# The last group's rows dealt to four column chunks: every fourth row, loaded by sixteen turns, stored and read back in 3328-byte pieces

## The chip, the cores and the metric

The kernel runs on one core of a Trainium2 chip. The metric is the time of one execution on the device in microseconds (us), the median of several runs. Beside these runs there is one execution taken with the hardware profiler; "the span" is the time from its first to its last instruction.

## The reference

A cross network (DCN) with six layers over 16384 rows of 416 bf16 features:

```python
B, F, D, L = 16384, 26, 16, 6          # Din = F * D = 416
def reference(x0, ws, bs):
    x = x0
    for l in range(L):
        proj = jnp.einsum('bd,de->be', x, ws[l]) + bs[l]
        x = x0 * proj + x
    return x
```

The inputs are `x0` of 16384 x 416, `ws` of 6 x 416 x 416 and `bs` of 6 x 416; the output has the shape of `x0`.

## The kernel before

The rows are cut into eight groups of 2048 (GC), each group into four chunks of 512 columns (NJ = 4, CH = 512). Inside the core a group stands transposed: features on the partitions, rows along the free dimension. The 416 features are three tiles of 128 (NT = 3) and a tail of 32. The tails of the four chunks share one tile of 128 partitions, one quadrant of 32 partitions to a chunk.

**Loading.** `load_group(g)` transposes a group while it loads it, by DMA transposes from the SP queue, here called turns. Each turn takes 2048 rows of 128 features: one for each feature tile (L408), and one of the last 128 features into a buffer `Tb`, which shares its memory with the output buffer `ost` (L413). Four small DMAs (L420) then copy the tails from `Tb` to their quadrants, and for some groups two more DMAs (L445, L446) write a rotated copy of the tails. The input buffers are five slots used in turn; group 7, the last, uses slot 2. Its load is queued when group 2 has been done with.

**Computing.** Jobs are pairs of group and layer. Matmuls for most of the run are issued in an order written out by hand (`ORDER`, replayed by `replay` and `stream`). A chunk's result is moved from PSUM by ScalarE with the bias added (L551), multiplied with x0 by VectorE (L563) and added to x (L568). The buffers of x are a pool of six (`xs`), those of the tails a pool of ten; a buffer that a finished group gives back is taken by a later job. The small rotations of tails (L445, L446) between layers also go through SP.

**Output of groups 0 to 4.** `output(g)` turns the finished features back to rows by four DMA transposes within SBUF (`turn`, L892, and `turn_rest`, L899), GpSimd spreads the tails (L922), and `store` writes the 2048 rows (L929). A row is 832 bytes. For group 0, whose rows were dealt to partitions four at a time when it was loaded, a partition writes 3328 bytes in one piece; for the other groups a piece is one row.

**The last layer of group 7.** It is computed the other way round, with rows on the partitions, so that no turn is needed after it. The group is handled in row blocks `kk` = 0 to 3, each with four PSUM banks j = 0 to 3: ScalarE copies a bank to `on` (L1189), VectorE multiplies with x0 in row-major form, `x0n7` (L1195), and adds x in row-major form, `x5n` (L1201), and `nat_store` writes the rows (L1208). Blocks 0 to 2 are one store each, block 3 is a store of half a block and two of a quarter. Group 6's last half is stored (L929) between them.

**Row-major x0.** `load_last()` reads group 7's x0 a second time, as rows (L870, four DMAs of 0.416 MB), into slot 3, and the last layer's bias (L874, four small DMAs). It is called when group 3 has been done with, right behind that group's turns and store in SP's queue. `on` uses slot 4, `x5n` slot 0.

A column of chunk j stands for a row of the group: with c the column's number in the chunk, before it is row 512 j + c.

The wait counts, and which engine waits for what, are worked out by `Program` from the names of tiles that each operation reads and writes; every engine's queue keeps the order in which operations were added.

Of the kernel before, what the change touches and what calls it, by code (L numbers as in the profile page):

```python
# [3 lines left out]
P = 128  # L4
CH = 512
# [16 lines left out]
class Program:  # L22
# [12 lines left out]
    def add(self, eng, fn, reads=(), writes=(), lane=None, batch=None, hold=False, release=False, row=None):  # L35
        op = Op(eng, fn, lane, batch, row)
        deps = {}
        if eng == "pool":
            writes = list(writes) + ["pool"]
        for t in reads:  # L40
            w = self.writer.get(t)
            if w is not None:
                deps[id(w)] = (w, True)
        for t in writes:
            w = self.writer.get(t)
            if w is not None:
                deps[id(w)] = (w, True)
            for r in self.readers.get(t, ()):
                if id(r) not in deps:
                    deps[id(r)] = (r, False)  # L50
        for d, raw in deps.values():
            if d.lane is None and d.eng == eng and lane is None and (eng == "pe" or not raw):
                if row is None or d.row is None or row == d.row:
                    continue
            op.deps.append(d)
        for t in reads:
            self.readers.setdefault(t, []).append(op)
        for t in writes:
            self.writer[t] = op
            self.readers[t] = []  # L60
        if eng == "dve":
            if hold:
                self.flush()
                self.held = op
            else:
                self.queue[eng].append(op)
                if release:
                    self.flush()
        else:
            self.queue[eng].append(op)  # L70
        if lane is not None:
            batches = self.lanes.setdefault(lane, [])
            if not batches or batches[-1][0] != batch:
                batches.append((batch, []))
            batches[-1][1].append(op)
        return op
# [230 lines left out]
def bass_standalone__cross_network_dcn__recsys_kernel(  # L307
# [6 lines left out]
    B, D = x0.shape  # L314
    L = ws.shape[0]
    NT = 3
    NJ = 4
    GC = NJ * CH
    NG = B // GC
    KK = CH // P  # L320
    assert D == NT * P + T32 and B == NG * GC and NG == 8 and L == 6
    LAST = NG - 1
# [10 lines left out]
    n = 0  # L333
# [6 lines left out]
    XW = NT * GC  # L340
# [7 lines left out]
    x0s = [nc.alloc_sbuf_tensor(f"x0_{s}", [P, XW + 2 * CH], BF16) for s in range(NX0)]  # L348
# [4 lines left out]
    ost = nc.alloc_sbuf_tensor("ost", [P, GC // P, D], BF16)  # L353
    Tb = ost[:, :, :].rearrange("p a f -> p (a f)")[:, 0:GC]
# [4 lines left out]
    add = pr.add  # L359
# [4 lines left out]
    def x0_tok(s, t, j):  # L364
        return ("x0", s, t, j)

    def x0_all(s):
        return [x0_tok(s, t, j) for t in range(NT) for j in range(NJ)] + [("x03r", s), ("x03r", s, "b")]
# [4 lines left out]
    def slot(g):  # L373
        return g % NX0
# [29 lines left out]
    def load_group(g):  # L404
        s = slot(g)
        rows = slice(g * GC, (g + 1) * GC)
        def turn(t):
            add("sp", lambda h: h.dma_start_transpose(  # L408
                x0s[s][:, t * GC:(t + 1) * GC], x0[rows, t * P:(t + 1) * P]),
                writes=[x0_tok(s, t, j) for j in range(NJ)], lane=f"x0_{s}_{t}", batch=g)  # L410

        turn(0)
        add("sp", lambda h: h.dma_start_transpose(Tb, x0[rows, D - P:D]),  # L413
            writes=[("ost", t, j) for t in range(NT + 1) for j in range(NJ)], lane="Tb", batch=g)
        turn(1)
        turn(2)
        if g > 1:
            for j in range(NJ):
                q = slice(j * T32, (j + 1) * T32)
                add("sp", lambda h, q=q, j=j: h.dma_start(  # L420
                    x0s[s][q, XW:XW + CH], Tb[P - T32:P, j * CH:(j + 1) * CH]),
                    reads=[("ost", 0, 0)], writes=[("x03q", s, j)], lane=f"x03_{s}", batch=g)
            rotate_x03(g)

    def rotate_x03(g):
        s = slot(g)
        if turn_of(g, 1):
            rotate(x0s[s][:, XW:XW + CH], x0s[s][:, XW + CH:XW + 2 * CH], turn_of(g, 1),
                   x03_toks(s), ("x03r", s), f"x03r_{s}", g)

    def x03_toks(s):
        return [("x03q", s, j) for j in range(NJ)]
# [23 lines left out]
    def x_src(g, l):  # L456

        if l == 0:
            s = slot(g)
            return lambda t, a, b: x0s[s][:, t * GC + a * CH:t * GC + b * CH], lambda t, j: x0_tok(s, t, j)  # L460
        s = xset[(g, l)]
        return lambda t, a, b: xs[s][:, t * GC + a * CH:t * GC + b * CH], lambda t, j: ("x", s, t, j)
# [8 lines left out]
    def done_with(g, l):  # L471
        users[(g, l)] = users.get((g, l), 0) + 1
        if users[(g, l)] < 2:
            return
        if l > 0:
            free_x.append(xset[(g, l)])
            free_3.append(xtail[(g, l)])
        if (g, l + 1) not in filled:
            prefill(g, l + 1)
        if l == L - 1:  # L480
            output(g)
            if g == 3:
                load_last()
            if 4 < g + NX0 <= LAST:
                later.append(g + NX0)
# [133 lines left out]
    def prefill(g, l):  # L619

        if 0 < l < L and turn_of(g, 1) and (g, l) != (LAST, L - 1):
            so = free_3.pop(0)
            xtail[(g, l + 1)] = so
            n = (turn_of(g, l + 1) - turn_of(g, l)) % NJ
            rotate(x3s[xtail[(g, l)]], x3s[so], n, [("x3", xtail[(g, l)])], ("x3", so), f"rot{so}", (g, l))
# [46 lines left out]
    def tails(batch, corners_last=False, banks=None):  # L672
# [42 lines left out]
        for g, l in batch:  # L715
            done_with(g, l)
        while later:
            load_group(later.pop(0))
# [6 lines left out]
        out=ident[:, :], in_=ident[:, :], compare_op=ALU.not_equal, fill=1.0, base=0,  # L725
# [8 lines left out]
    def load_nat(j, k0, k1):  # L734
# [6 lines left out]
        reads=["warm"], writes=["warm"])  # L741
# [6 lines left out]
    load_w3(0, "sp")  # L748
    load_wm(0, "sp", W0, D)
    load_group(1)  # L750

    def second_tails():
# [108 lines left out]

    view = "p (j k f) -> p j k f"
    sn, so, s5 = slot(3), slot(4), slot(5)
    x0n7, x5n, on = (x0s[s][:, 0:XW + CH].rearrange(view, j=NJ, k=KK) for s in (sn, s5, so))
    rows7 = x0[LAST * GC:B, :]

    def load_last():

        for j in range(NJ):
            add("sp", lambda h, j=j: h.dma_start(  # L870
                x0n7[:, j, :, :], rows7[j * CH:(j + 1) * CH, :].rearrange("(k p) f -> p k f", k=KK)),
                writes=(x0_all(sn) + x03_toks(sn) if j == 0 else []) + [("n7", j)], lane="n7", batch=0)
        for j in range(NJ):
            add("sp", lambda h, j=j: h.dma_start(brow[j * T32:j * T32 + 1, :], bs[L - 1:L, :]),  # L874
                reads=["brow"], writes=[("brow", j)], lane="brow", batch=0)

    def output(g):

        s, s3 = xset[(g, L)], xtail[(g, L)]
        if g < LAST - 2:  # L880
            turn(g, 0)
            turn_rest(g)
            spread("pool")
            turn(g, 1)
            turn(g, 2)
            store(g, 0, NJ)
        free_x.append(s)
        free_3.append(s3)
# [72 lines left out]
    k = 0  # L961
# [17 lines left out]
    def start_job(g, l, ahead=True):  # L979
        started.add((g, l))  # L980
        if ahead:
            xset[(g, l + 1)] = free_x.pop(0)
        if (g, l) in W_LOAD:
            load_wm(W_LOAD[(g, l)], "sp")
            load_w3(W_LOAD[(g, l)], "sp")
        if (g, l) in G_LOAD:
            load_group(G_LOAD[(g, l)])
# [141 lines left out]
    g, l = LAST, L - 1  # L1129
    src, stok = x_src(g, l)  # L1130
# [61 lines left out]
    def nat_mul(kk, j, n=2):  # L1192
        o, x0v = on[:, j:j + n, kk, :], x0n7[:, j:j + n, kk, :]
        toks = [("on", a, kk) for a in range(j, j + n)]
        add("dve", lambda h: h.tensor_tensor(o, o, x0v, ALU.mult),  # L1195
            reads=toks + [("n7", a) for a in range(j, j + n)], writes=toks)

    def nat_add(kk, j, n=2):
        o, x5v = on[:, j:j + n, kk, :], x5n[:, j:j + n, kk, :]
# [4 lines left out]
    stores = [0]  # L1204

    def nat_store(kk, j0, j1, eng="sp"):
        dst = out[LAST * GC:B, :].rearrange("(j k p) f -> p j k f", j=NJ, k=KK)[:, j0:j1, kk, :]
        add(eng, lambda h: h.dma_start(dst, on[:, j0:j1, kk, :]),  # L1208
            reads=[("on", j, kk) for j in range(j0, j1)],
            writes=[("out7", kk, j0)], lane=f"out7_{stores[0]}", batch=0)  # L1210
        stores[0] += 1
# [18 lines left out]
    for j in (0, 2):  # L1230
        nat_mul(0, j)
    for j in (0, 2):
        nat_add(0, j)
    nat_store(0, 0, NJ)
    store(LAST - 1, 2, NJ)
    for kk in range(1, KK):
# [48 lines left out]
```

## Time and profile before

| what | us |
|---|---|
| median of 3 runs | 466.94 |
| lowest and highest | 466.86, 467.11 |
| the profiled execution | 467.6 |
| its span | 465.8 |
| busy: TensorE, VectorE, ScalarE, GpSimd | 459.0, 402.9, 382.3, 6.9 |
| first and last start of L408 turns | 7.4, 285.3 |
| from issue to landing: L408, L413, L899 (median) | 5.2, 6.0, 2.6 |
| from issue to landing: stores L929, L1208 (median) | 7.1, 4.3 |

TensorE's granted clock was 0.998 over the span. The DMA engines moved 53.78 MB, a mean of 115 GB/s; of 139152 packets 112826 are under 512 bytes, most of them the turns' 256. In views of the trace, "SPq" and "ACTq" are the DMA issues of SP and ScalarE; the time beside such a line is how long the issue held the queue, not how long the data took. "DMA share" is the mean busy share of the 16 DMA engines in a stretch; it can stand a little above 1, since packets overlap.

### The profile page before, as it was taken

The page shows a single profiled execution, that of the slowest core. Times are in us where ns is not written, and L with a number is a line of the kernel's source. Part 1 is how long each engine was busy: PE and PEld are TensorE (multiplying, and loading weights), DVE is VectorE, ACT ScalarE, POOL GpSimd, SP SyncE. Part 2 cuts the span into 40 slices and gives each one's busy share as a digit, 9 for nine tenths or more (in the row PEclk, how much of TensorE's full clock was granted, in tenths as well). Part 3 has the DMA queues.
Part 4 walks back from the last instruction along what each step waited for, and adds up shares of the span by engine and source line. Part 5 has one row for each costly group of instructions (what it writes and reads, how often), then busy time and mean ns, then how long its engine had stood idle before and what let it go on. Part 6 is the DMA issues. An engine that isn't in the chain of part 4 may idle for free.

```text
span 465.8 us, 17814 instructions
## 1 busy us (share of the span) xinstructions
PE 459.0 (99%) x8001; PEld 265.9 (57%) x8001; DVE 402.9 (87%) x696; ACT 382.3 (82%) x609; POOL 6.9 (1%) x15
## 2 busy tenths in 40 slices
PE   9999999999999999999999999999999999999994
PEld 5344656575655556555665556565556665556552
DVE  1887898988889898898988979898988988989996
ACT  4686889887988888897888889888888897989794
POOL 1000000000000000000000000000000000000000
PEclk9999999999999999999999999999999999999999
DMA  8985859000002859095568619983000084182999
GB/s 229 185 177 120 176 118 193 10 23 12 16 4 37 152 172 189 13 143 167 110 120 126 183 36 177 132 239 115 25 2 4 25 148 149 37 137 82 184 177 275
DMA packets 139152, 53.78 MB, mean 115 GB/s; under 512 B 112826, under 2 KB 138564, under 8 KB 139076
## 3 DMA queue, kind: packets, MB, share of 16 engines
q1 hardware_dynamic: 138920, 52.54, 52.8%
q8 instruction: 62, 1.02, 0.9%
q10 hardware_dynamic: 156, 0.11, 0.1%
q14 instruction: 14, 0.11, 0.1%
HBM read 5.97 MB, written 13.63 MB: 42 GB/s over the span
## 4 chain that ended last, share of the span: by engine, by line
PE 96%; DVE 2%; ACT 1%; issue 0%; DVEq 0%
PE ps L1075 73%; PE ps L692 7%; PE ps L1079 6%; PE ps L645 5%; PE ps L639 1%; PE ps L680 1%; DVE x L1201 1%; DVE x L1195 1%; PE ps L772 1%; PE ps L790 1%; ACT tw L551 1%; PE ps L666 1%; DVE tw L563 0%; DVE x L568 0%; DVE x L1163 0%
## 5 line engine op out<-in xcount | busy, mean ns | idle before, releaser
L1075 PE MATMUL ps<-x,wm 32*128 32x512 bf16 x6288 | 372.9, 374 | 0.0
L551 ACT ACTIVATE tw<-ps,bias 128x512 bf16<-128x512 f32 x524 | 327.3, 688 | 48.6 <-PE ps L1075 35.9
L1075 PEld LDWEIGHTS ps<-x,wm 32*128 32x128 bf16 x6288 | 221.6, 92 | 136.0 <-ACT tw L551 6.5
L563 DVE TENSOR_TENSOR tw<-tw,x 128x1024 bf16<-128x1024 bf16 x262 | 176.6, 687 | 41.5 <-ACT tw L551 40.0
L568 DVE TENSOR_TENSOR x<-tw,x 128x1024 bf16<-128x1024 bf16 x262 | 171.0, 688 | 0.3
L1079 PE MATMUL ps<-x,w 32*128 32x512 bf16 x524 | 159.3, 374 | 0.0
L1079 PEld LDWEIGHTS ps<-x,w 32*128 32x128 bf16 x524 | 44.6, 92 | 6.1
L692 PE MATMUL ps<-x,wm 128*32 128x512 bf16 x564 | 33.6, 380 | 0.0
L612 ACT ACTIVATE ts<-ps,bias 128x512 bf16<-128x512 f32 x32 | 20.4, 686 | 13.1 <-PE ps L680 13.1
L515 ACT ACTIVATE tw<-ps,bias 128x1024 bf16<-128x1024 f32 (+1 forms) x24 | 20.7, 938 | 8.1 <-PE ps L666 7.0
L692 PEld LDWEIGHTS ps<-x,wm 128*32 128x32 bf16 x564 | 13.5, 96 | 18.2 <-ACT tw L551 3.7
L645 PE MATMUL ps<-x,wm 128*128 128x512 bf16 x92 | 21.6, 384 | 0.0
L616 DVE TENSOR_TENSOR x<-ts,x 128x512 bf16<-128x512 bf16 x47 | 18.4, 418 | 0.3
L645 PEld LDWEIGHTS ps<-x,wm 128*128 128x128 bf16 x92 | 8.4, 98 | 11.7 <-issue 2.3
L524 DVE TENSOR_TENSOR tw<-tw,x 128x1024 bf16<-128x1024 bf16 (+1 forms) x21 | 13.0, 636 | 2.2 <-ACT tw L515 2.1
L608 DVE SCALAR_TENSOR_TENSOR ts<-ps,bias,x 128x512 bf16<-128x512 f32 x15 | 11.2, 747 | 3.1 <-PE ps L680 3.1
L529 DVE TENSOR_TENSOR x<-tw,x 128x1024 bf16<-128x1024 bf16 (+1 forms) x21 | 12.6, 633 | 0.0
L614 DVE TENSOR_TENSOR ts<-ts,x 128x512 bf16<-128x512 bf16 x32 | 12.4, 417 | 0.0
L922 POOL COPY ost<-ot 128x512 bf16<-128x512 bf16 x6 | 5.5, 912 | 390.8 <-DMA ot<-x 390.8
L800 DVE COPY x<-ps 128x512 bf16<-128x512 bf16 x5 | 2.0, 423 | 8.6 <-PE ps L790 8.6
L1140 PE MATMUL ps<-wm,x 128*128 128x416 bf16 x48 | 9.3, 340 | 0.0
L1189 ACT ACTIVATE x<-ps 128x416 bf16<-128x416 f32 x16 | 7.7, 528 | 1.5 <-PE ps L1140 1.5
(51 smaller groups left out, 72.7 us busy)
## 6 DMA issues: line engine op xcount, KB each, us to landing
out_dram<-ost SPq DMA_DIRECT2D x6, 1664.0 KB, 7.8
x<-x SPq DMA_DIRECT2D x24, 96.0 KB, 2.2
x<-in_x_dram SPq DMA_DIRECT2D x8, 208.0 KB, 4.5
x<-in_x_dram SPq DMA_DIRECT2D x4, 416.0 KB, 8.3
out_dram<-ost SPq DMA_DIRECT2D x2, 832.0 KB, 4.2
wm<-in_ws_dram SPq DMA_DIRECT2D x5, 312.0 KB, 3.4
x<-x SPq DMA_DIRECT2D x22, 64.0 KB, 2.2
out_dram<-x SPq DMA_DIRECT2D x3, 416.0 KB, 4.9
```

The source lines that it names most:

```text
L515: add("act", lambda h, a=a, w=w, b0=b0: h.activation(tw[r][:, a * CH:(a + w) * CH], psum[:, b0 * CH:(b0 + w) * CH], ACT_F.Identity, bias=b ...
L524: add("dve", lambda h, a=a, e=e: h.tensor_tensor(tw[r][:, a * CH:e * CH], tw[r][:, a * CH:e * CH], x0s[s0][:, i * GC + a * CH:i * GC + e * ...
L529: add("dve", lambda h, a=a, e=e: h.tensor_tensor(xs[so][:, i * GC + a * CH:i * GC + e * CH], tw[r][:, a * CH:e * CH], src(i, a, e), ALU.ad ...
L551: add("act", lambda h: h.activation(tw[r][:, j * CH:(j + 1) * CH], bank(b), ACT_F.Identity, bias=bias[:, i, l:l + 1], scale=1.0), reads=[( ...
L563: add("dve", lambda h: h.tensor_tensor(tw[r][:, o], tw[r][:, o], x0s[s0][:, c], ALU.mult), reads=[("tw", r, k) for k in both] + [x0_tok(s0 ...
L568: add("dve", lambda h: h.tensor_tensor(xs[so][:, c], tw[r][:, o], src(i, a, a + 2), ALU.add), reads=[("tw", r, k) for k in both] + [stok(i ...
L612: add("act", lambda h: h.activation(ts[r][:, :], bank(b), ACT_F.Identity, bias=bias[:, 3, l:l + 1], scale=1.0), reads=[("ps", b), "bias"], ...
L616: add("dve", lambda h: h.tensor_tensor(x3s[so][:, :], ts[r][:, :], res, ALU.add), reads=[("ts", r)] + rtok, writes=[("x3", so), ("x3", so, ...
L645: add("pe", lambda h, t=t, j=j: h.matmul(bank(banks[j]), wm[l][:, t, ecols], src(t, j, j + 1), start=(first and t == 0), stop=(not first a ...
L692: add("pe", lambda h, t=t, j=j, src=src, l=l, b=b, ro=ro, qo=qo: h.matmul(psum[qo, b * CH:(b + 1) * CH], wm[l][:, t, NT * P:D], src(t, j, ...
L1075: add("pe", lambda h, l=l, t=t, j=j, b=b, q=q, ecols=ecols, src=src, kw=kw: h.matmul(bank(b), wm[l][q, t, ecols], src(t, j, j + 1)[q, :], ...
L1079: add("pe", lambda h, l=l, b=b, q=q, ecols=ecols, s3=s3, kw=kw: h.matmul(bank(b), w3[l][q, ecols], s3[q, :], **kw), reads=tok3 + [("w3", l ...
```

## The change

Group 7's rows are dealt out anew: column c of chunk j is now row 4 c + j of the group. So a partition of a row block holds four neighbouring rows in its four banks.

For this the group's load takes every fourth row: each of its four turns becomes four, of 512 rows each, one to a chunk, with a stride of four rows in DRAM (16 turns in all). `x0n7` and `on` change their layout in SBUF, so that the four rows of a partition stand side by side, 3328 bytes; `x5n` keeps its own. `load_last` now makes one DMA for each row block, with 128 pieces of 3328 bytes, and is called when group 4 has been done with, not group 3. `nat_store` writes a partition's rows in one piece: 3328 bytes for row blocks 0 to 2, 1664 for the first half of block 3, 832 as before for its last two quarters. VectorE's multiply at L1195 names all four of the row-major loads as read.

```diff
     def load_group(g):
...
+        by4 = x0[rows, :].rearrange("(q j) f -> j q f", j=NJ)
+
         def turn(t):
-            add("sp", lambda h: h.dma_start_transpose(
-                x0s[s][:, t * GC:(t + 1) * GC], x0[rows, t * P:(t + 1) * P]),
-                writes=[x0_tok(s, t, j) for j in range(NJ)], lane=f"x0_{s}_{t}", batch=g)
+            if g < LAST:
+                add("sp", lambda h: h.dma_start_transpose(
+                    x0s[s][:, t * GC:(t + 1) * GC], x0[rows, t * P:(t + 1) * P]),
+                    writes=[x0_tok(s, t, j) for j in range(NJ)], lane=f"x0_{s}_{t}", batch=g)
+                return
+            for j in range(NJ):
+                add("sp", lambda h, j=j: h.dma_start_transpose(
+                    x0s[s][:, t * GC + j * CH:t * GC + (j + 1) * CH], by4[j, :, t * P:(t + 1) * P]),
+                    writes=[x0_tok(s, t, j)], lane=f"x0_{s}_{t}", batch=g)
+
+        def turn_b(j0, j1, src):
+            add("sp", lambda h: h.dma_start_transpose(Tb[:, j0 * CH:j1 * CH], src),
+                writes=[("Tb", j) for j in range(j0, j1)] + (
+                    [("ost", t, j) for t in range(NT + 1) for j in range(NJ)] if j0 == 0 else []), lane="Tb", batch=g)
 
         turn(0)
-        add("sp", lambda h: h.dma_start_transpose(Tb, x0[rows, D - P:D]),
-            writes=[("ost", t, j) for t in range(NT + 1) for j in range(NJ)], lane="Tb", batch=g)
+        if g < LAST:
+            turn_b(0, NJ, x0[rows, D - P:D])
+        else:
+            for j in range(NJ):
+                turn_b(j, j + 1, by4[j, :, D - P:D])
         turn(1)
         turn(2)
...
             output(g)
-            if g == 3:
+            if g == 4:
                 load_last()
...
-    x0n7, x5n, on = (x0s[s][:, 0:XW + CH].rearrange(view, j=NJ, k=KK) for s in (sn, s5, so))
+    x5n = x0s[s5][:, 0:XW + CH].rearrange(view, j=NJ, k=KK)
+    x0n7, on = (x0s[s][:, 0:XW + CH].rearrange("p (k j f) -> p j k f", j=NJ, k=KK) for s in (sn, so))
...
-        for j in range(NJ):
-            add("sp", lambda h, j=j: h.dma_start(
-                x0n7[:, j, :, :], rows7[j * CH:(j + 1) * CH, :].rearrange("(k p) f -> p k f", k=KK)),
-                writes=(x0_all(sn) + x03_toks(sn) if j == 0 else []) + [("n7", j)], lane="n7", batch=0)
+        for k in range(KK):
+            add("sp", lambda h, k=k: h.dma_start(
+                x0n7[:, :, k, :], rows7[k * CH:(k + 1) * CH, :].rearrange("(p j) f -> p j f", j=NJ)),
+                writes=(x0_all(sn) + x03_toks(sn) if k == 0 else []) + [("n7", k)], lane="n7", batch=0)
...
     def nat_store(kk, j0, j1, eng="sp"):
-        dst = out[LAST * GC:B, :].rearrange("(j k p) f -> p j k f", j=NJ, k=KK)[:, j0:j1, kk, :]
+        dst = out[LAST * GC:B, :].rearrange("(k p j) f -> p j k f", j=NJ, k=KK)[:, j0:j1, kk, :]
```

More of the change, by code (lines that the diff above doesn't have):

```diff
@@ L421, in load_group @@
                     x0s[s][q, XW:XW + CH], Tb[P - T32:P, j * CH:(j + 1) * CH]),
-                    reads=[("ost", 0, 0)], writes=[("x03q", s, j)], lane=f"x03_{s}", batch=g)
+                    reads=[("ost", 0, 0), ("Tb", j)], writes=[("x03q", s, j)], lane=f"x03_{s}", batch=g)
             rotate_x03(g)
@@ L1195, in nat_mul @@
         add("dve", lambda h: h.tensor_tensor(o, o, x0v, ALU.mult),
-            reads=toks + [("n7", a) for a in range(j, j + n)], writes=toks)
+            reads=toks + [("n7", k) for k in range(KK)], writes=toks)
     def nat_add(kk, j, n=2):
```

## The prediction

> **What bounds the kernel now.** I read the page first, for who carries the span.
>
> ```profile
> PE 459.0 (99%) x8001; PEld 265.9 (57%) x8001; DVE 402.9 (87%) x696; ACT 382.3 (82%) x609; POOL 6.9 (1%) x15
> ...
> PE 96%; DVE 2%; ACT 1%; issue 0%; DVEq 0%
> ```
>
> TensorE is busy 99% of the span and makes up 96% of the chain that ended last. The program's TensorE, VectorE, ScalarE and GpSimd queues hold the same operations in the same order after the change, so nothing up to about 446 us moves unless a transfer comes late. That leaves two places: the end, where no matmul runs any more, and SP's queue, where the transfers are issued. For the end I read the windows.
>
> ```profile
> core 0: us, PE busy (x) PEld busy (x) DVE busy (x) ACT busy (x) POOL busy (x), PEclk, DMA share, GB/s
> 163.00:166.00 3.00, 3.00 (x68) 1.28 (x59) 2.75 (x5) 1.95 (x4) 0.00 (x0) 1.00 1.01 399
> 307.00:310.00 3.00, 3.00 (x61) 1.97 (x56) 2.76 (x6) 2.65 (x6) 0.00 (x0) 1.00 1.05 347
> 459.00:464.00 5.00, 0.75 (x5) 0.20 (x2) 2.39 (x8) 1.28 (x3) 0.00 (x0) 1.00 1.07 343
> ```
>
> The last two columns matter. From 459 to 464 the 16 DMA engines are full (share 1.07) at 343 GB/s. What they move are stores in 832-byte pieces: the second half of group 6 (L929, issued at 457.37) and the row-major stores of the last group (L1208). The row at 307 is another 832-byte store, of group 3, at 347 GB/s. The row at 163 is group 0's store, the only one in 3328-byte pieces: 399 GB/s. The last arithmetic is VectorE's at 461.4, the last data packet ends at 464.6, the span ends at 465.8. So it is the drain of the stores that sets the last four microseconds.
>
> For the queue I read SP's timeline around the group 7 load.
>
> ```profile
> 277.32 2.13 SPq L408 DMA_TRANSPOSE x<-in_x_dram  x1
> 279.50 2.43 SPq L413 DMA_TRANSPOSE ost<-in_x_dram  x1
> 281.98 5.91 SPq L408 DMA_TRANSPOSE x<-in_x_dram  x2
> 287.93 3.34 SPq L420 DMA_DIRECT2D x<-ost  x4
> ...
> 293.74 2.82 SPq L892 DMA_TRANSPOSE ost<-x  x1
> 296.60 1.27 SPq L899 DMA_TRANSPOSE ot<-x  x1
> 297.91 5.05 SPq L892 DMA_TRANSPOSE ost<-x  x2
> 305.83 0.39 SPq L929 DMA_DIRECT2D out_dram<-ost  x1
> 306.27 5.56 SPq L870 DMA_DIRECT2D x<-in_x_dram  x4
> ```
>
> The load's four turns hold SP for 10.6 us, and group 3's output turns (L892, L899) follow with no pause: whatever the load gains in length, they inherit.
>
> **The stores.** Six stores of L1208 change. The first (row block 0) is issued at 454.53, ahead of the half-group L929 store, whose packets start only at 458.3 because it is issued at 457.37; a faster first store leaves a longer gap there and moves nothing. From 458.3 the drain is unbroken. Row blocks 1 and 2 are 0.426 MB each: 1.242 us at 343 GB/s, 1.068 us at 399, so 0.17 us saved on each. The first half of row block 3 goes from 832 to 1664-byte pieces: 0.213 MB, 0.62 us now; no store in the trace has that size, so its gain lies between 0 and 0.09 us (the 3328-byte rate), and I take 0.07, since it is nearer the long piece in what it saves of piece count (a half against three quarters). The last two stores hold one row of 832 bytes per partition as before: nothing. Sum 0.42 us, if the drain stays unbroken: the last store is issued by ScalarE at 461.46, and L929 shows 0.9 us from issue to first packet, so it is ready at 462.4, before its turn comes at about 463.5. It is still the drain that ends last. VectorE's multiplies and adds over 832 elements (L1195, L1201, 0.59 us) read one run instead of two; they were at the pace of the 1024-element L563 already (0.69 us), so I give them nothing.
>
> The Trainium skill ("DMA: Bandwidth & Descriptors", section "Where 436 GB/s comes from") speaks against most of this: it holds that transfers between HBM and SBUF are bound near 358 GB/s per core. By that, the 1.065 MB above would go from 3.11 to 2.97 us, an estimate of 0.13 us saved. The 399 GB/s row of this trace disagrees with it, and I go by the row.
>
> **The sixteen turns.** Four turns of 2048 rows become sixteen of 512. No row shows a 512-row turn from DRAM. The nearest is L899, a turn of 128x512 within SBUF: 1.19 us least, 1.27 median, 2.14 most, the last behind a full queue. The bounds: a 512-row turn as a quarter of the shortest whole L408 (1.67/4 = 0.42 us), or as costly as a whole one here (2.6). I take the median, since the packets of a quarter turn need only about a quarter of 2.6 = 0.65 us of the DMA engines, so the queue behind it shouldn't fill. With the 0.04 us between issues: 16 x 1.31 = 21.0, so SP is 10.4 us later at L420 and after. Ends: earlier by 3.2, at 0.46 each, if the engines' 0.65 does not hold it back to about no change; later by 31 at 2.6.
>
> Who notices 10.4 us? Matching the trace's records to the queues in order:
> Group 7's inputs are first read by TensorE at 315.4. The last turn would be issued by 298.3 and landed by 301 to 304 (2.6 us as L899, 6.1 as now). Covered.
> Group 3's output turns land at 298.6, 304.2 and 305.8. VectorE overwrites what they read in the L568 operations that start at 314.43, 317.84 and 320.27. At 10.4 us later 5.4, 3.3 and 4.1 us are left. Covered; the tightest cover ends at 13.7 us.
> The rotation of group 7's tails (L445, L446 at 292.56) is wanted by VectorE at about 329. Covered. GpSimd's copy (L922) waits for the L899 turn and goes with it, and has nothing behind it until 377. Group 3's store (305.83) goes to 316.2; the output buffer is wanted at 372.
>
> **The residual load.** L870 and L874 (4 + 4 DMAs, 7.5 us of SP) move from behind group 3's store to behind group 4's, past the two pairs of rotations at 313.83 to 316.40, the pairs at 330, 331, 363 and 365, and group 4's turns and store (372.28 to 384.0). The rotations at 313.83 would be issued at 316.7 instead (10.4 later, 7.5 earlier) and wait behind 5 us of group 3's store; they land near 324 and are first wanted at 329.9. At the new place the eight DMAs run from 384.0 to at most 391.6; SP's next operation waits for VectorE until 395.57. Their data follow group 4's store, which lands at 392.0, and need 4.3 us at 399 GB/s; the first reader is L1195 at 452.4. Nothing moves there. The rotations at 395.57 may land a microsecond later; they are wanted from 420.
>
> **Sum.** The profiled execution took 467.6 us with a span of 465.8, 0.7 above the median of the runs. 467.6 - 0.42 = 467.2; on the median, 466.94 - 0.42 = 466.5 us.
>
> **Rivals.** *The drain is no faster.* 399 GB/s was seen with nothing behind it in the queue; at the end small stores and two issuing engines mix. Then the time is 466.9. For it: 832-byte stores too differ by their moment, 347 GB/s at 307 and 308 GB/s between 385.5 and 390. Against: 399 holds for three steady microseconds. 0.15. The Trainium skill's bound (same page and section) would make it 466.8, an estimate.
>
> *A quarter turn is dear* (the other side). One mechanism: SP's delay makes group 3's output turns land after VectorE wants their buffer; VectorE stands at L568 at 317.84 with the L563 multiplies queued behind it; ScalarE's L551 finds its result buffer unread (it reuses them from 7.2 us after); then no PSUM bank comes free and TensorE stands. VectorE waits from a mean of 1.52 us per turn (16 m - 10.6 > 13.7), TensorE from about 1.97 (7.2 more). At 2.18, the dearest L899 row plus its gap, the loss is 16 x 2.18 - 10.6 - 13.7 - 7.2 = 3.4 us: 469.9 us. At 2.6 it is 10: 477. For it: that one row, and that L892 took up to 4.3 us when turns were queued. Against: six of the seven L899 rows are at most 1.71. 0.12, with 0.03 more for a loss in another place that I do not see. It ends slower than before by 0.2% only from a mean of about 2.05 us.
>
> *More than the drain.* If the shorter end also let the half-group store start earlier, which I see no way for, or the freed DMA engines at 307 to 318 helped: over 0.93 us faster, 0.05.
>
> *The change doesn't do what it says*: if a store in the new layout were still cut in 832-byte pieces the result is the first rival's; the built program names 128x1664 for it, so I fold it in there.
>
> **How the numbers follow.** Forecast 0.65, drain no faster 0.15, dear turns 0.12 and elsewhere 0.03, much faster 0.05. 0.2% is 0.93 us, about what a measurement of this kernel can tell from no change; the forecast and the first rival both lie within it: same 0.80, slower 0.15, faster 0.05. The range: below, twice the saving, 466.1; above, no gain and half a microsecond of a stall begun, 467.5. It holds the forecast and the first rival.
>
> **What would show it.** In the profile after: SP's timeline with sixteen turns at about 1.3 us and L892 of group 3 near 304; VectorE's L568 at 314 to 320 with no wait on a DMA; the windows from 459 on near 370 GB/s with the share still full; the last data near 464.2. A TensorE gap near 318 or a VectorE wait there would make the second rival right; a drain at 343 GB/s the first.

## The result and the profile after

The changed kernel takes 466.35 us (median of 17 runs, 465.94 to 466.98) where the kernel before took 467.14 on the same chip (17 runs, 466.86 to 467.47): ratio 0.9983, 95% interval 0.9976 to 0.9991, so 0.4 to 1.1 us faster. The profiled execution took 466.98 us with a span of 465.2, 0.6 us less than before. Line numbers after L404 are higher in the changed kernel, by 8 at first (L408 is L416, L413 is L421), then by 16 (L420 is L436, L568 is L584, L608 is L624) and by 17 (L892 is L909, L929 is L946, L1208 is L1225).

From the page of the changed kernel, the engines' busy time (first line of part 1):

```profile
PE 458.9 (99%) x8001; PEld 267.2 (57%) x8001; DVE 403.3 (87%) x696; ACT 381.9 (82%) x609; POOL 7.2 (2%) x15
```

Nothing in the computation has moved. The windows of the changed kernel, with the DMA share and GB/s in the last two columns:

```profile
core 0: us, PE busy (x) PEld busy (x) DVE busy (x) ACT busy (x) POOL busy (x), PEclk, DMA share, GB/s
307.00:310.00 3.00, 3.00 (x64) 1.93 (x61) 2.76 (x5) 2.64 (x6) 0.00 (x0) 1.00 0.96 184
459.00:464.00 5.00, 0.70 (x4) 0.20 (x2) 2.34 (x7) 1.23 (x3) 0.00 (x0) 0.99 1.05 376
```

The row at 459 is the one that the change was about: the engines are about as full as before (1.05 and 1.07) and carry 376 GB/s instead of 343. At 307 the store of group 3 is gone, it now comes at 317.8, and turns run in its place. SP's timeline of the changed kernel shows why:

```profile
277.43 5.19 SPq L416 DMA_TRANSPOSE x<-in_x_dram  x4
282.66 5.71 SPq L421 DMA_TRANSPOSE ost<-in_x_dram  x4
288.41 11.90 SPq L416 DMA_TRANSPOSE x<-in_x_dram  x8
300.36 3.28 SPq L436 DMA_DIRECT2D x<-ost  x4
...
306.12 2.06 SPq L909 DMA_TRANSPOSE ost<-x  x1
308.22 1.71 SPq L916 DMA_TRANSPOSE ot<-x  x1
309.97 4.50 SPq L909 DMA_TRANSPOSE ost<-x  x2
317.83 0.40 SPq L946 DMA_DIRECT2D out_dram<-ost  x1
```

Sixteen turns hold SP from 277.43 to 300.36, 1.43 us each; the copies behind them come 12.4 us later than before, group 3's store 12.0. VectorE's timeline of the same stretch has no wait on a DMA at the three L584 operations:

```profile
314.73 1.28 DVE L584 TENSOR_TENSOR x<-tw,x 128x1024 bf16<-128x1024 bf16 x2
...
317.94 1.29 DVE L584 TENSOR_TENSOR x<-tw,x 128x1024 bf16<-128x1024 bf16 x2
...
320.34 1.29 DVE L584 TENSOR_TENSOR x<-tw,x 128x1024 bf16<-128x1024 bf16 x2
```

It is close, though: the third of group 3's output turns lands at 317.81, and VectorE starts at 317.94.

### The profile page after: what moved, and what is told of

It is laid out like the page before. It is cut to its first block, busy times and chain, and to the rows that moved or that the text cites. A ratio compares the mean times of both kernels' runs of the same rounds, so it can differ in the third digit from the quotient of the medians.

```text
span 465.2 us, 17826 instructions
## 1 busy us (share of the span) xinstructions
PE 458.9 (99%) x8001; PEld 267.2 (57%) x8001; DVE 403.3 (87%) x696; ACT 381.9 (82%) x609; POOL 7.2 (2%) x15
## 4 chain that ended last, share of the span: by engine, by line
PE 94%; DVE 2%; DMA 1%; ACT 1%; SPq 1%; issue 0%; DVEq 0%
PE ps L1092 73%; PE ps L708 7%; PE ps L1096 6%; PE ps L661 4%; PE ps L655 1%; PE ps L696 1%; DMA x<-in_x_dram 1%; DVE x L1218 1%; DVE x L1212 1%; ACT tw L567 1%; PE ps L682 1%; SPq L751 0%; DVE tw L579 0%; DVE x L584 0%; PE ps L806 0%
## 5 line engine op out<-in xcount | busy, mean ns | idle before, releaser
L584 DVE TENSOR_TENSOR x<-tw,x 128x1024 bf16<-128x1024 bf16 x262 | 171.2, 689 | 0.3
L661 PEld LDWEIGHTS ps<-x,wm 128*128 128x128 bf16 x92 | 8.5, 98 | 11.5 <-issue 2.3
L624 DVE SCALAR_TENSOR_TENSOR ts<-ps,bias,x 128x512 bf16<-128x512 f32 x15 | 11.2, 747 | 3.1 <-PE ps L696 3.1
L630 DVE TENSOR_TENSOR ts<-ts,x 128x512 bf16<-128x512 bf16 x32 | 12.4, 418 | 0.0
```

Of the source, the lines that this page charges most:

```text
L584: add("dve", lambda h: h.tensor_tensor(xs[so][:, c], tw[r][:, o], src(i, a, a + 2), ALU.add), reads=[("tw", r, k) for k in both] + [stok(i ...
L661: add("pe", lambda h, t=t, j=j: h.matmul(bank(banks[j]), wm[l][:, t, ecols], src(t, j, j + 1), start=(first and t == 0), stop=(not first a ...
```

## Experiments

The theory: the whole gain is the drain of the stores at the end, through the size of their pieces; the turns and the moved residual load cost and bring nothing, because they are covered. The rivals: the gain comes from the moved residual load, or the turns cost something that hides a larger gain. A second group of kernels asks how much cover there is. Ratios are to the kernel before on the same chip, with 95% intervals. In the first group that kernel took 467.26 us, in the second 467.10, in the third 467.40.

### Which part gains

**The changed kernel again** (`again`).

> The changed kernel once more, on the same chip as the three beside it. Theory (the drain): only the stores after 458.3 us gain; the trace after shows 0.5 us there, so 0.4 to 0.6 us faster than before, ratio about 0.9989. Rival (something besides the drain gains, for example the residual load that no longer runs beside group 3's store): 0.8 us or more, ratio 0.9983 or less, as the first 17 runs gave.

466.55 us, 0.9985 (0.9977 to 0.9994), span 465.2. The difference of the medians, 0.7 us, lies between the two expectations.

**Short pieces** (`short`): the changed kernel, `on` as it was.

```diff
-    x5n = x0s[s5][:, 0:XW + CH].rearrange(view, j=NJ, k=KK)
-    x0n7, on = (x0s[s][:, 0:XW + CH].rearrange("p (k j f) -> p j k f", j=NJ, k=KK) for s in (sn, so))
+    x5n, on = (x0s[s][:, 0:XW + CH].rearrange(view, j=NJ, k=KK) for s in (s5, so))
+    x0n7 = x0s[sn][:, 0:XW + CH].rearrange("p (k j f) -> p j k f", j=NJ, k=KK)
```

> The changed kernel with `on` laid out as before, so that every store of the last group goes in 832-byte pieces again; the dealt rows, the sixteen turns, the moved residual load and its 3328-byte pieces stay. Theory (the drain): the gain goes, ratio to before 0.9995 to 1.0005, and the windows from 459 to 464 are back at 343 GB/s. Rival (the gain comes from the moved load or from the turns): it keeps most of its gain, ratio 0.9985 or less with a drain at 343 GB/s.

467.21 us, 0.9997 (0.9989 to 1.0006). The gain is gone; its interval and that of `again` still overlap a little, so the drain has to bear it out. In this profile the drain began at 457.3, 0.9 us earlier than in that of the kernel before, so the window is shifted:

```profile
458.00:463.00 5.00, 1.21 (x7) 0.48 (x5) 2.85 (x8) 1.73 (x4) 0.00 (x0) 0.89 1.07 343
```

343 GB/s again, as the theory had it. VectorE's multiplies and adds of the last layer take a median of 0.58 to 0.59 us in the kernel before, in the changed one and in `short`, so the layout gains nothing there. Dealt rows, sixteen turns and the moved load are all in this kernel and bring nothing that can be seen.

**The residual load back behind group 3** (`early`).

```diff
-            if g == 4:
+            if g == 3:
                 load_last()
```

> The changed kernel with the residual load back behind group 3's store. Theory (the drain): nobody waits for those transfers in either place, so the time is that of the changed kernel within 0.1 us; SP's rotations of 318 us go to about 324 and land near 331, where VectorE wants the first at 329.8, so a wait of VectorE of about a microsecond may show, without a cost at the end. Rival (the move of the load is what gains): the time of before, or up to 1 us over it.

466.52 us, 0.9987 (0.9978 to 0.9995): the time of the changed kernel. Its drain:

```profile
458.60:463.60 5.00, 0.61 (x4) 0.12 (x2) 2.25 (x7) 1.14 (x3) 0.00 (x0) 0.90 1.04 375
```

and VectorE's waits between 322 and 336, in the order engine, line, what it waited for, us, times, longest:

```profile
DVE tw L579 <- ACT tw L567: 1.0, 3, 0.5
DVE x L632 <- DMA x<-x: 0.9, 1, 0.9
```

The second line is the wait of a microsecond for the late rotation. It costs nothing at the end. Where the load stands is not what gains.

**The turns alone** (`turns`): the kernel before, with group 7's four turns cut in four, neighbouring rows.

```diff
...
+            for j in range(NJ):
+                add("sp", lambda h, j=j: h.dma_start_transpose(
+                    x0s[s][:, t * GC + j * CH:t * GC + (j + 1) * CH], part(j)[:, t * P:(t + 1) * P]),
+                    writes=[x0_tok(s, t, j)], lane=f"x0_{s}_{t}", batch=g)
...
```

> The kernel before with one part of the change alone: group 7 is loaded by sixteen turns of 512 rows, but neighbouring rows, so the dealing, the layouts, the stores and the residual load are as before. Theory: the sixteen turns are covered; SP reaches L420's copies about 12 us later as in the changed kernel (a mean of 1.43 us a turn, whatever the stride of the rows), the time is that of before within 0.1 us, although the rotations behind the residual load now come some 12 us later too (near 326, wanted at 329.8). Rival (the turns cost something that the changed kernel's stores hide): 0.2 to 0.5 us slower than before.

467.39 us, 1.0009 (0.9998 to 1.0020): a cost between nothing and 0.9 us, which this interval does not settle. Sixteen turns of neighbouring rows took 22.9 us of SP (277.17 to 300.02), those of every fourth row in the changed kernel 22.9 as well: the stride cost nothing here.

The trace's packets give the drain to the hundredth in all of these kernels. From the first packet of group 6's second half to the end of the last: 6.42 us in the kernel before, 6.42 in `short`, 6.43 in `turns`; 5.87 in the changed kernel, in `again` and in `early`. From the last packet's end to the end of the span: 1.10, 1.11 and 1.10 against 0.97, 0.90 and 0.97. So 0.55 us are the drain, and 0.13 to 0.2 more come behind it.

### How much cover there is

Three kernels make the delay of SP longer by more turns in group 7's load, into a free part of the output buffer; their results are not used, but the tail copies wait for them. They stand ahead of the last eight of the load's sixteen turns, so half of group 7's inputs come later too.

```diff
                 turn_b(j, j + 1, by4[j, :, D - P:D])
+            spare = ost[:, :, :].rearrange("p a f -> p (a f)")
+            for n in range(3):
+                add("sp", lambda h, n=n: h.dma_start_transpose(
+                    spare[:, GC + n * 512:GC + (n + 1) * 512], by4[n % NJ, 0:512, D - P:D]),
+                    writes=[("spare", n)], lane="spare", batch=g)
...
```

**Three more** (`dose3`).

> The changed kernel with three more turns of 512 rows in group 7's load, into a part of the output buffer that is free then. SP comes 4.3 us later still: 12.4 + 4.3 = 16.7 us. The prediction's covers: VectorE waits from 13.7 us on, so here some 2 to 3 us in all at the L568 operations of 314 to 320; TensorE only from 20.9: the time stays that of the changed kernel within 0.2 us. Rival (the covers are worth nothing more once VectorE waits): 2 to 3 us slower.

**Eight more** (`dose8`).

> The same with eight more turns: SP 12.4 + 11.5 = 23.9 us later. By the prediction's sum VectorE waits about 10 us and TensorE stands for 23.9 - 20.9 = 3 us: 3 us slower than the changed kernel, 469 to 470. Rival (VectorE's lost time is made up by its idle share, and the first reader among TensorE's matmuls is 13 us and more behind): under 1 us slower. Rival on the other side (every later microsecond counts from 13.7): 10 us slower.

**Sixteen more, of 256 rows** (`dose16`).

> The same with sixteen more turns, of 256 rows each. If such a turn holds SP as long as one of 512 rows (1.3 us, a fixed cost), SP is 12.4 + 21 = 33 us later: by the prediction's sum 12 to 13 us slower than the changed kernel, near 479, and TensorE's first read of group 7 at 315.4 still only just covered. If the time goes with the rows (0.7 us), 12.4 + 11 = 23.5 us later and the time is that of the kernel with eight more turns.

| kernel | group 3's store issued, later than before by | time, us | over the changed kernel (466.55) |
|---|---|---|---|
| `again` | 14.2 | 466.55 | |
| `dose3` | 17.5 | 471.49 | 4.9 |
| `dose8` | 22.4 | 478.04 | 11.5 |
| `dose16` | 33.9 | 489.16 | 22.6 |

The medians are of 4, 4 and 2 runs. The expectations drawn from the prediction (no change, 3, 12 to 13) were all wrong, and the rival of `dose3` (2 to 3 us) was too low as well; that of `dose8` (10 us) came nearest. From `dose3` to `dose16` 16.4 us of delay cost 17.7 us, though not by one path, as shown below. `dose3`, whose profile is of its slowest run (472.55 us), is decided by these waits between 316 and 334:

```profile
DVE x L589 <- DMA ost<-x: 6.4, 2, 4.1
...
PEld ps L1097 <- DVE ts L629: 4.3, 1, 4.3
PE ps L1097 <- DVE ts L629: 3.8, 1, 3.8
```

VectorE waits for the output turns as the rival said, but TensorE does not come to stand through ScalarE. It waits for VectorE itself: L629 (L608 before) reads a tail's PSUM bank with VectorE. VectorE's timeline of `dose3`:

```profile
316.81 1.29 DVE L589 TENSOR_TENSOR x<-tw,x 128x1024 bf16<-128x1024 bf16 x2 [2.32 <-DMA ost<-x]
...
323.44 1.29 DVE L589 TENSOR_TENSOR x<-tw,x 128x1024 bf16<-128x1024 bf16 x2 [4.13 <-DMA ost<-x]
...
331.27 0.74 DVE L629 SCALAR_TENSOR_TENSOR ts<-ps,bias,x 128x512 bf16<-128x512 f32 x1
```

and in the kernel before:

```profile
327.13 0.74 DVE L608 SCALAR_TENSOR_TENSOR ts<-ps,bias,x 128x512 bf16<-128x512 f32 x1
```

The operation that ended at 327.87 now ends at 332.01. TensorE's next matmul into that bank stood at 328.10 before, 0.2 us behind, and stands at 332.07 here.

TensorE's stand of 3.8 us is not the whole loss: the span is 5.5 us over that of the changed kernel (470.7 against 465.2). The windows of `dose3` show the rest:

```profile
330.00:340.00 10.00, 7.93 (x116) 4.05 (x119) 8.01 (x16) 5.07 (x9) 0.00 (x0) 0.83 0.13 36
340.00:350.00 10.00, 10.00 (x191) 5.76 (x188) 9.42 (x16) 8.69 (x15) 0.00 (x0) 1.00 0.01 3
```

The third number from the end is the granted clock. Its mean falls to 0.83 behind the stand; in the trace it is 0.5 from 333.03 to 336.44, and 3.4 us at half the clock lose the missing 1.7.

`dose8` and `dose16` hold other paths besides. Waits in `dose8` between 310 and 345:

```profile
PE ps L1097 <- DVE ts L629: 5.8, 1, 5.8
ACT tw L572 <- DVE x L589: 4.7, 2, 3.8
PEld ps L1097 <- ACT tw L572: 3.4, 2, 3.3
```

and in `dose16` between 310 and 350:

```profile
PE ps L1097 <- DMA x<-in_x_dram: 9.5, 2, 5.4
PEld ps L1097 <- DVE ts L629: 6.3, 1, 6.3
```

In `dose8` TensorE also stood 2.8 us through ScalarE, whose L572 waited for VectorE's L589: the prediction's path, here beside the other. In `dose16` 9.5 us of its stands are waits for group 7's own inputs, which the expectation had as just covered. So these two kernels tell what a long delay costs, not that the one bank costs it.

**That one tail on ScalarE** (`tail_act`): `dose3` with the tail bank of job (4,4) emptied by ScalarE.

```diff
-                evacuate_tail(*batch[k], bs_[k], vector=k == 1)
+                evacuate_tail(*batch[k], bs_[k], vector=k == 1 and batch[k] != (4, 4))
```

> The kernel with three more turns (471.5 us, 0.9 to 1.0% over before), with one thing changed: the tail bank of job (4,4), which VectorE empties itself, L608 in the kernel before, 327.1 to 327.9, and TensorE wants 0.2 us later, is emptied by ScalarE here, as its two neighbours are. Theory (VectorE's wait reaches TensorE through this one bank): TensorE's gap of 3.8 us at 332 goes or shrinks below 1 us, VectorE's waits on the output turns stay at about 6 us, and the time falls to 467.5 or less. Rival (it reaches TensorE through ScalarE's result buffers or the input of the next job, as the prediction's sum had it): it stays near 471.

467.04 us, 0.9995 (0.9982 to 1.0008), where `dose3` had 1.0091 (1.0070 to 1.0111). Its waits between 316 and 334:

```profile
DVE x L589 <- DMA ost<-x: 4.1, 1, 4.1
ACT tw L572 <- DVE x L589: 0.9, 1, 0.9
PEld ps L1097 <- ACT ts L633: 0.7, 1, 0.7
```

VectorE still waits 4.1 us here and 0.5 just before 316 (4.6 in all, where about 6 was expected), and TensorE's stand of 3.8 has shrunk to a gap of 0.4, with its clock at 1.00 throughout. In this profile the third output turn landed 1.6 us earlier than in that of `dose3`; that alone would have left a stand of some 2.2 us (an estimate, 3.8 - 1.6). So the path of `dose3` is shown: one bank, emptied by the engine that was made to wait. What is left over the changed kernel, 0.5 us, lies within the intervals.

The same path is at work, small, in the changed kernel itself. Its second profile (`again`), waits between 313 and 331:

```profile
DVE x L584 <- DMA ost<-x: 2.1, 1, 2.1
...
PEld ps L1092 <- DVE ts L624: 0.8, 1, 0.8
```

There the third output turn landed at 320.05, not 317.81, and VectorE waited 2.1 us; its idle time before L624 took up most of that, and TensorE lost 0.3.

### Can the end be shorter still

The DMA engines have nothing to do between 457.9 and 458.3, because group 6's second half waits for its last turn, while row block 1 has been ready since 456.7. `swap` issues row block 1 first; `bswap` does the same to the kernel before; `half` stores row block 1 in two halves as well.

```diff
     nat_store(0, 0, NJ)
-    store(LAST - 1, 2, NJ)
...
         if kk < last:
             nat_store(kk, 0, NJ)
+        if kk == 1:
+            store(LAST - 1, 2, NJ)
```

and for `half`, besides:

```diff
                 nat_add(kk, j - 1)
+                if kk == 1:
+                    nat_store(kk, j - 1, j + 1)
...
-        if kk < last:
+        if 1 < kk < last:
             nat_store(kk, 0, NJ)
```

> The changed kernel with one order changed on SP: the store of row block 1 is issued before the store of group 6's second half, not after it. Theory (the drain sets the end from 456 us on, and the gap of some 0.4 us in the DMA engines at 457.9 to 458.3 is only there because the half-group store waits for its last turn): row block 1 is ready at 456.7, its packets fill the gap, and the end comes 0.4 to 0.7 us sooner than in the changed kernel, ratio to before about 0.997 to 0.998. Rival (the end hangs on the last store's own way from its issue at 461.4, not on the queue of data): no gain over the changed kernel.

> The kernel with the store of row block 1 ahead of group 6's second half once more, beside two of its relatives. First it gave 0.9981 where the changed kernel gave 0.9985 on the same chip, with intervals that overlap. Theory (the idle stretch of the DMA engines before 458.3 is the end's): 0.3 to 0.5 us under the changed kernel's 466.5, ratio 0.9972 to 0.9980. Rival (no gain): 0.9985.

> The kernel before with that swap of two stores alone, 832-byte pieces, nothing dealt anew. Theory: the swap and the long pieces are separate gains of the same queue of data, so here some 0.3 to 0.5 us faster than before, ratio 0.9990 to 0.9994. Rival (only with long pieces is there an idle stretch worth filling): no change, 0.9997 to 1.0003.

> The swap, and row block 1 stored in two halves of 1664-byte pieces, the first as soon as its two banks are done (a microsecond earlier). Theory: the DMA engines' idle half microsecond at 457 goes too, 0.2 to 0.3 us under the swap alone. Rival: the shorter pieces (69 ns against half of 135) and one more issue on SP, 0.6 to 1.2 us each, take it back: the swap's time or 0.2 us over it.

| kernel | time, us | ratio to before | 95% interval |
|---|---|---|---|
| `swap` | 466.14 | 0.9981 | 0.9972 to 0.9990 |
| `swap_again` | 466.50 | 0.9983 | 0.9974 to 0.9992 |
| `bswap` | 467.08 | 0.9999 | 0.9990 to 1.0007 |
| `half` | 466.23 | 0.9980 | 0.9971 to 0.9989 |

Each of the intervals overlaps that of the changed kernel, 0.9977 to 0.9994. In the profiles the idle stretch is shorter (`swap`, 0.24 us) or gone (`swap_again`, `bswap`, `half`), the spans of `swap`, `swap_again` and `half` are 464.6, 464.0 and 464.4 against 465.2, and the engines carry more between 455 and 458. The changed kernel:

```profile
455.00:458.00 3.00, 3.00 (x24) 1.38 (x23) 2.93 (x6) 2.07 (x4) 0.00 (x0) 1.00 0.96 257
```

and `swap_again`:

```profile
455.00:458.00 3.00, 3.00 (x24) 1.40 (x22) 2.90 (x6) 2.39 (x5) 0.00 (x0) 1.00 1.06 324
```

`bswap` decides nothing: its interval holds the theory's 0.9990 to 0.9994 as well as the rival's 0.9997 to 1.0003, and the ratio on record is not the quotient of the two medians, which would be 0.9993. A gain of 0.1 to 0.4 us is possible for `swap` and `half`, less than the 0.4 to 0.7 that was expected of `swap`, and `swap_again` (0.9983) lies by its rival (0.9985) rather than its theory (0.9972 to 0.9980). The gain is not shown: single executions differ by a microsecond, and VectorE's wait at L584 (1.7 us in `swap`, 1.9 in `half`) is in them too. `swap` and `half` beat the kernel before; that they beat the changed one stays open.

## Why the prediction was right, and where it was not

**The forecast** was 466.5 us, 0.42 under the kernel before; measured were 466.35 and, the second time, 466.55. That the time came so close is partly luck: the sum started from 466.94, but beside the changed kernel the one before took 467.14, and the gain was 0.79 us (0.71 in `again`), nearly twice the 0.42. The two errors go against each other. The mechanism was the right one: `short` takes the long pieces away and the gain goes, `early` and `turns` show that no other part brings it.

**The size of the drain's term** was 0.42 us; by the packets it is 0.55, with 0.13 to 0.2 more behind the last packet, together about 0.7 of the 0.7 to 0.8 that the medians show. Row blocks 1 and 2 saved 0.17 and 0.16 (from first packet to first packet), as worked out. The term that was mis-sized is row block 3, where the sum had 0.07 for the first half and "nothing" for the two quarters: from its first packet to the end of the last it took 1.46 us and now 1.30 (1.29 in `again`), 0.16 less. How that divides can't be read, since the packets of ScalarE's quarter run between those of the half (in the kernel before they start at 463.59, the half's last ends at 464.08). The shorter way behind the last packet had no term at all. The last data packet ended at 464.70 before, not at 464.6 as read, and at 464.21 after. Why these went faster was not tried. The rate of the long pieces held: 128 packets of 1664 bytes at 69 ns each, those of 3328 at 137. The Trainium skill's bound of about 358 GB/s ("DMA: Bandwidth & Descriptors", section "Where 436 GB/s comes from") would have left a saving of 0.13 us, an estimate; the trace disagrees with it, since the 376 GB/s from 459 to 464, nearly half of that time still on short pieces, lie above it.

**The turns** were put at 1.31 us with the gap, from L899's median; they took 1.43, since three of the sixteen took 1.8 to 2.1 instead of 1.26. So the delay at the copies was 12.4 us, not 10.4.

**The cover** is where the prediction's reading was wrong, though the time didn't suffer. It compared each output turn's landing with the L568 that overwrites what it read and found 13.7 us at the tightest. But the second and third turn share one semaphore, so L568 at 317.84 waits for both: 305.82 against 317.84, 12.0 us. The delay of the store was 12.0 in the first profile and 14.2 in the second, and 10.6 to 13.7 in the six others with just the sixteen turns, so the changed kernel stands on that edge, not 3.3 us inside it.

**The second rival's price** was wrong by more. The path by which ScalarE wants a result buffer, a further 7.2 us on, exists (TensorE's 2.8 us in `dose8`), but it is not the first. Behind the waiting L568 stands L608, and TensorE wants its bank 0.2 us after it; all that lies between is VectorE's own idle time, some 1.2 us from 318 to 327. So TensorE loses from a delay of about 13 to 14 us, where the sum said 20.9. And the sum had no term for the clock, which in `dose3` made 5.5 us out of a stand of 3.8. At 2.18 us a turn, 24.3 us later, the rival would have cost not 3.4 but some 13 us, an estimate between `dose8` (11.5 us at 22.4) and `dose16` (22.6 at 33.9). It would have begun at a mean of about 1.5 us a turn, not 1.97. No run lies between the 14.2 us of `again`, with no cost that can be seen, and the 17.5 of `dose3` with 4.9, so at which mean the kernel would be slower by 0.2% stays open; at the 2.05 of the sum SP would be 22.2 us later, where `dose8` lost 11.5. With 1.43 measured, the chance of 0.12 was too small.

**The first rival**, a drain no faster, is refuted by the 376 GB/s. The **residual load** went as predicted: its eight DMAs ran from 383.99 to 390.74 and nobody noticed; the rotations at 313.83 were issued at 318.27, landed from 324.8 and were wanted at 329.8.

## What to carry to other kernels

In this kernel, whose end is a queue of stores with full DMA engines, the bytes of a piece set the end, and only there: the same longer pieces in the residual load, for which no engine waited, bought nothing. Before transfers are made longer ahead of others in a queue, ask of the engine that would wait not only what it waits for next, but every instruction queued behind that wait, and look first for one that frees a PSUM bank. A cover is read from the semaphore's last contributor, not from the transfer that one has in mind. And a stand of TensorE is priced with the stretch at half clock that may follow it.

## What the runs showed of the hardware

A DMA transpose's issue on SP did not go with its rows between 256 and 512: the shortest held SP 1.24 us at 256 rows and 1.26 at 512. `dose16`, SP's timeline:

```profile
288.23 23.52 SPq L433 DMA_TRANSPOSE ost<-in_x_dram  x16
```

23.52 / 16 = 1.47 us, against 1.43 for those of 512. A whole turn of 2048 rows took 2.6 (1.67 the shortest). Stores went at 343 GB/s in pieces of 832 bytes at the end (347 and 308 in two earlier stretches of the kernel before), and at 399 to 404 in pieces of 3328 (group 0's store, in the two profiles). After a stand of 3.8 us (`dose3`) TensorE was granted half its clock for 3.4 us; after stands of 0.4 and 0.3 us (`tail_act`, `again`) it kept 1.00.
